# A linear-attention and two-MLP kernel: weight units confined to chunks 2 to 4, casts pinned to later steps, first weights converted in two parts

## The chip, the core and the metric

The kernel runs on one core of a Trainium2 chip, as one program from inputs in memory to outputs in memory. The metric is the device time of that program in microseconds. Of the engines, TensorE (PE) multiplies matrices, VectorE (DVE) and ScalarE (ACT) do elementwise work, GpSimd (POOL) and SyncE (SP) mostly issue DMAs. Each engine works through its own list of instructions in order and waits on semaphores of the others.

## What is computed

Three layers, one after the other, on 4 x 576 = 2304 tokens of width 512. Q, K and V have 8 heads of 64; the weights of both MLPs come in 64-bit floats and are turned to 32 bits on the chip.

```python
def _attn_ref(q, k, v):                       # each head, each batch
    q_s = exp(q - max(q, -1)); q_s /= sum(q_s, -1) + 1e-09
    k_s = exp(k - max(k, 2));  k_s /= sum(k_s, 2) + 1e-09      # over the sequence
    kv = einsum('bhsd,bhse->bhde', k_s, v)
    return einsum('bhsd,bhde->bhse', q_s, kv)

def _moe_ref(x, w_in, w_out, s, b):           # first MLP, 512 -> 2048 -> 512
    r = maximum(x @ w_in, 0.0)
    return (s * (r * r) + b) @ w_out

def _moe2_ref(x, w_in, w_out):                # second MLP, 512 -> 2048 -> 512
    h = x @ w_in
    return (h * tanh(softplus(h))) @ w_out
```

## The kernel before

**Chunks and steps.** The tokens are cut into five chunks of 512, 256, 512, 512 and 512 (chunks 0 to 4). Per chunk the attention of four pairs of heads (hp 0 to 3) gives four x tiles, and the first MLP then runs in 16 steps of 128 of its 2048 inner columns: step n is one h (a matmul group over four x tiles, kk 0 to 3), a relu and a square on ScalarE, and one y group into four accumulators. So there are 80 steps, 16 to a chunk. The attention of the next chunk is spread over the steps of this one. After the last chunk the second MLP runs on pairs of chunks, with products P1 to P7 of half blocks (seven multiplications of blocks in place of eight), and a rest.

**Halves.** A 32-bit matmul is done in three passes: each operand is split into a rounded high part and the remainder, by a cast on ScalarE and a subtraction on VectorE (`split`, L170 and L167). Names show it: xh and xl, gh and gl, kvh and kvl. Only the first steps of chunk 0 multiply whole operands (t, x), because their weights have not been split yet: h up to step 8, y up to step 6.

**Weights of the first MLP.** A pair of 128 x 512 blocks j is loaded by SP (`load_w`, tiles raw), its 64-bit words are turned to 32 bits by `bits` (L129 on ScalarE, then L130, L133, L137 and L141 on VectorE, in place in tile t), and later split into w. Tile t of j lies where the raw words of j - 1 were.

**Units.** The weights of the second MLP are cut into 32 units. A unit is one load of 512 KB (`unit_load`, tile ur, L302), the same five `bits` steps on a 512-wide tile u, four sums of blocks (L313), two casts and two subtractions into one tile umem, and two stores by GpSimd (L326, to wdi or wdo). `STARTS` holds the half step at which each unit begins: three from step 23 on, in chunk 1, and 29 over steps 32 to 78. The later ring of weight tiles (rw, `ring_load` on GpSimd's queue) reads back what the units stored.

**Second MLP's x.** In the last chunk `b_next` is called seven times for each of two k halves (tiles b_0 and b_1), from step L0 + 1 and from L0 + 7; L0 is the first step of the last chunk. Each call combines y blocks and splits one operand into xoP.

**What sets the order.** The program hands its instructions to a scheduler that orders each engine's list by a modelled time. `pin` and `keep_in_program_order` keep an instruction at its place in the program on its engine; unit casts, unit bits and the relus from step 23 (`U1`) on are pinned, x casts, kv casts and xoP casts are not. `at(step, kind, fn)` puts work into steps; within a step `run` names the kinds in order.

## Time and profile before

| | us |
|---|---|
| median of 3 runs | 865.53 (864.23 to 865.64) |
| the profiled execution | 868.49, its span 866.7 |
| TensorE busy | 828.4 (96%) |
| VectorE busy | 616.9 (71%) |
| ScalarE busy | 440.8 (51%) |
| GpSimd busy | 109.3 (13%) |
| mean granted TensorE clock | 0.988 of full |

The busy times are sums over the span, and the engines work beside each other. The granted clock is what the chip gave TensorE: 1.00 is 2.4 GHz and 0.50 is 1.2 GHz. A timeline row's bracket tells how long its engine had been idle before it and whose work ended that. The chunks follow each other in the span: chunk 0 until about 147 us, chunk 1 until about 213, chunks 2 to 4 until about 495, then the second MLP.

### The profile page before, as it was taken

The numbers are of one execution on the slowest core, as the hardware profiler recorded it, in microseconds if no ns is written. First come the engines' busy times: TensorE is split into PE (matmuls) and PEld (weight loads), VectorE is DVE, ScalarE is ACT, GpSimd is POOL, SyncE is SP. The second block draws the span as 40 slices with busy tenths as digits, with TensorE's granted clock in tenths as the row PEclk, the third lists the DMA queues.
The fourth block names the chain that finished last, engine by engine and source line by source line (L and its number), as shares of the span: only waits on it lengthen the run. The fifth ranks groups of instructions, "written<-read, shape, count | busy, mean of one in ns | idle before, by whom it ended". The sixth has DMA issues, their size and how long they took to land.

```text
span 866.7 us, 11570 instructions
## 1 busy us (share of the span) xinstructions
PE 828.4 (96%) x4084; PEld 666.0 (77%) x4084; DVE 616.9 (71%) x1153; ACT 440.8 (51%) x786; POOL 109.3 (13%) x196
## 2 busy tenths in 40 slices
PE   3799999998999999999989999989999999999998
PEld 2344787987888888888868878868788888878897
DVE  6989997568888887766887448687864655786511
ACT  3645777547666666555765435255442333544322
POOL 4000000000011001120212211101111111112110
PEclk9899999998999999999999999999999999999999
DMA  6994123144666556456656889657678866687891
GB/s 170 311 376 143 27 66 112 54 103 149 207 199 205 191 196 220 165 182 216 217 186 202 272 244 374 201 189 242 220 233 281 250 177 223 217 280 262 255 375 68
DMA packets 90474, 179.02 MB, mean 207 GB/s; under 512 B 26928, under 2 KB 45104, under 8 KB 86832
## 3 DMA queue, kind: packets, MB, share of 16 engines
q0 software_dynamic: 30256, 112.73, 40.0%
q1 hardware_dynamic: 59072, 64.50, 24.2%
q10 hardware_dynamic: 1088, 1.05, 0.4%
q8 instruction: 32, 0.52, 0.3%
q14 instruction: 26, 0.21, 0.1%
HBM read 131.60 MB, written 46.66 MB: 206 GB/s over the span
## 4 chain that ended last, share of the span: by engine, by line
PE 69%; DVE 13%; DMA 11%; SPq 2%; issue 2%; ACT 2%; POOL 0%; DVEq 0%; ACTq 0%; POOLq 0%
PE P L177 22%; PE h L177 16%; PE y L177 16%; PE rh L177 3%; PE ry L177 3%; DMA q<-in_q_dram 2%; DMA raw<-in_moe_w_out_dram 2%; DVE g L348 2%; DMA kb<-in_k_dram 2%; DVE w L167 1%; DVE gly_P L167 1%; PE P3y L177 1%; PE P5y L177 1%; PE P7y L177 1%; PE P4y L177 1%
## 5 line engine op out<-in xcount | busy, mean ns | idle before, releaser
L177 PE MATMUL h<-xh,w 128*128 128x512 f32 (+1 forms) x568 | 177.6, 378 | 7.8 <-ACT r L240 4.2
L177 PE MATMUL y<-gh,w 128*128 128x512 f32 (+1 forms) x584 | 176.6, 369 | 0.0
L177 PE MATMUL P<-xoP,rw 128*128 128x512 f32 x672 | 155.2, 390 | 1.0 <-DMA rw<-wdi 1.0
L177 PEld LDWEIGHTS P<-xoP,rw 128*128 128x128 f32 x672 | 125.8, 188 | 27.3 <-issue 1.4
L177 PEld LDWEIGHTS h<-xh,w 128*128 128x128 f32 x568 | 106.2, 194 | 26.6 <-ACT r L240 4.9
L177 PEld LDWEIGHTS y<-gh,w 128*128 128x128 f32 x584 | 106.5, 188 | 17.8
L170 ACT CAST ghy_P<-g 128x512 fp32r<-128x512 f32 x112 | 69.7, 623 | 82.4 <-DVE gly_P L167 34.7
L455 DVE TENSOR_TENSOR s<-s,P 128x512 f32<-128x512 f32 x112 | 75.2, 684 | 47.7 <-PE P L177 38.3
L177 PE MATMUL h<-xl,w 128*128 128x512 f32 (+1 forms) x284 | 106.7, 376 | 0.4 <-DVE xl L167 0.4
L177 PE MATMUL y<-gl,w 128*128 128x512 f32 (+1 forms) x292 | 106.8, 369 | 0.0
L167 DVE TENSOR_TENSOR gly_P<-g,ghy_P 128x512 fp32r<-128x512 f32 x112 | 75.8, 688 | 40.1 <-ACT ghy_P L170 39.2
L177 PE MATMUL P<-ghy_P,rw 128*128 128x512 f32 x224 | 87.2, 391 | 0.0
L458 ACT ACTIVATE g<-s 128x512 f32<-128x512 f32 x64 | 39.9, 631 | 81.7 <-DVE s L455 81.4
L170 ACT CAST umem<-u 128x512 fp32r<-128x512 f32 x64 | 37.4, 619 | 51.4 <-DVE u L313 45.5
L177 PEld LDWEIGHTS h<-xl,w 128*128 128x128 f32 x284 | 55.1, 194 | 9.7 <-DVE xl L167 0.6
L177 PEld LDWEIGHTS y<-gl,w 128*128 128x128 f32 x292 | 55.0, 188 | 9.0 <-DVE gl L167 0.2
L240 ACT ACTIVATE r<-h 128x512 f32<-128x512 f32 (+1 forms) x80 | 44.0, 550 | 31.0 <-PE h L177 26.4
L167 DVE TENSOR_TENSOR gl<-r,gh 128x512 fp32r<-128x512 f32 (+1 forms) x73 | 45.7, 628 | 14.3 <-ACT gh L170 14.2
L167 DVE TENSOR_TENSOR umem<-u,umem 128x512 fp32r<-128x512 f32 x64 | 42.1, 685 | 9.9 <-ACT umem L170 9.6
L177 PEld LDWEIGHTS P<-ghy_P,rw 128*128 128x128 f32 x224 | 42.1, 188 | 8.2
L243 ACT ACTIVATE r<-r 128x512 f32<-128x512 f32 (+1 forms) x80 | 47.0, 588 | 1.9
L177 PE MATMUL P<-gly_P,rw 128*128 128x512 f32 x112 | 45.2, 404 | 2.1 <-DVE gly_P L167 1.7
(181 smaller groups left out, 1299.1 us busy)
## 6 DMA issues: line engine op xcount, KB each, us to landing
rw<-wdo POOLq DMA_DIRECT2D x28, 1024.0 KB, 5.1
wdi<-umem POOLq DMA_DIRECT2D x32, 512.0 KB, 3.6
wdo<-umem POOLq DMA_DIRECT2D x32, 512.0 KB, 4.3
rw<-wdi POOLq DMA_DIRECT2D x16, 1024.0 KB, 6.6
rw<-wdi POOLq DMA_DIRECT2D x16, 768.0 KB, 6.0
raw<-in_moe_w_in_dram SPq DMA_DIRECT2D x16, 512.0 KB, 10.0
raw<-in_moe_w_out_dram SPq DMA_DIRECT2D x16, 512.0 KB, 10.8
ur<-in_moe_w_in_dram SPq DMA_DIRECT2D x16, 512.0 KB, 4.1
```

The lines of the kernel that those rows point to most:

```text
L167: eng.tensor_tensor(out=lo, in0=src, in1=hi.bitcast(F32), op=ALU.subtract)
L170: pin(nc.scalar.copy(out=hi, in_=src))
L177: mm = nc.tensor.matmul(out=ps, lhsT=x, rhs=y, start=start, stop=stop)
L240: op = nc.scalar.activation(out=r, in_=h_ps.pop(m), func=AF.Relu)
L243: nc.scalar.activation(out=r, in_=r, func=AF.Square)
L348: nc.vector.tensor_tensor(out=t.rearrange("p (a b) n -> p b a n", b=2)[:, 1], in0=t[:, 1:3], in1=t[:, 0:1].to_broadcast([P, 2, CM]), op=AL ...
L455: nc.vector.tensor_tensor(out=out, in0=a, in1=b, op=ALU.add)
L458: nc.scalar.activation(out=g[:, spot], in_=src, func=AF.Mish)
```

## The change

It has five parts. All 32 units start in steps 32 to 77, evenly, 1.44 steps apart where it was 1.59, so that none but the loads and sums of the first lie in chunk 1; relus are pinned from step 32 on. The first four x casts and kv casts, with their subtractions, are pinned: one x pair at each of h steps 5 to 8 (it was all four at step 8, free to move), and one kv pair at each of steps 3 to 6 (it was 0 to 3, free). The first weights are turned by two calls of `bits`, each on one of the two blocks. The casts of the second MLP's x are pinned and begin at L0 + 2 and L0 + 7. The ring's first tiles are taken in another order and loaded at L0 + 6, 10 and 14.

```diff
-        bits(t, w_raw.pop(j))
+        raw = w_raw.pop(j)
+        if j:
+            bits(t, raw)
+        else:
+            for i in range(2):
+                bits(t[:, i], raw[:, i])
...
-    def minus(eng, lo, src, hi):
-        eng.tensor_tensor(out=lo, in0=src, in1=hi.bitcast(F32), op=ALU.subtract)
-
-    def split(hi, lo, src, eng=None, pin=lambda ins: None):
+    def minus(eng, lo, src, hi, pin=lambda ins: None):
+        pin(eng.tensor_tensor(out=lo, in0=src, in1=hi.bitcast(F32), op=ALU.subtract))
+
+    def split(hi, lo, src, pin=lambda ins: None, pin_lo=lambda ins: None):
         pin(nc.scalar.copy(out=hi, in_=src))
-        minus(eng or nc.vector, lo, src, hi)
+        minus(nc.vector, lo, src, hi, pin_lo)
...
     U0 = 2 * NF
-    U1 = U0 - 9
-    STARTS = [2 * U1, 2 * U1 + 6, 2 * U1 + 12] + [2 * U0 + 2 * (NS - 2 - U0) * e // 29 for e in range(29)]
+    STARTS = [2 * U0 + 2 * (NS - 2 - U0) * e // 32 for e in range(32)]
...
-        if m >= U1:
+        if m >= U0:
             tc.keep_in_program_order(op)
...
-        split(x_op[r][:, 0, kb], x_op[r][:, 1, kb], src)
+        split(x_op[r][:, 0, kb], x_op[r][:, 1, kb], src, pin=pin)
...
-    RING = ("ws0", "last", "ws1")
+    RING = ("last", "ws0", "ws1")
...
             if c == 1:
-                at(hp, "att1", kv_hi, 0, hp)
-                at(hp, "att1", kv_lo, 0, hp)
+                at(hp + 3, "att1", kv_hi, 0, hp, pin)
+                at(hp + 3, "att1", kv_lo, 0, hp, pin)
...
-    at(U1 - 3, "load", unit_load, 0)
+    at(U0 - 4, "load", unit_load, 0)
...
-            at(L0 + 1 + 6 * kb + i, "unit", b_next, kb)
-    for s in (9, 11, 13):
+            at(L0 + 2 + 5 * kb + i, "unit", b_next, kb)
+    for s in (6, 10, 14):
         at(L0 + s, "load", ring_load)
...
-            if m == H_WHOLE - 1:
-                for kk in range(NK):
-                    x_t[0, kk] = tuple(t[:, 0:CHUNKS[0]] for t in x_tiles(kk, f"0_{kk}"))
-                    split(*x_t[0, kk], x_whole[kk])
+            if H_WHOLE - 1 - NK < m < H_WHOLE:
+                kk = m - H_WHOLE + NK
+                x_t[0, kk] = tuple(t[:, 0:CHUNKS[0]] for t in x_tiles(kk, f"0_{kk}"))
+                split(*x_t[0, kk], x_whole[kk], pin, pin)
```

`kv_hi` and `kv_lo` pass their new argument on to the cast and to the subtraction. Lines behind L170 stand four or five lines further down in the changed kernel (L240 is L244).

Three places show what the scheduler makes of it. On ScalarE at the start, before the first weights (t_295, from raw_172), the list before was this; xh, kvh are casts of x and kv halves, q_2 an exponential.

```order
L170 CAST xh_0_642<-x_247 128x512
L795 CAST kvh_1_464<-kvb_129 128x128
L745 ACTIVATE q_2_146<-q_2_146 128x640
L838 COPY x_293<-x_1_291 128x512
L816 COPY qt_341<-qt_2_331 128x512
L170 CAST xh_1_646<-x_293 128x512
L129 ACTIVATE t_295<-raw_172 128x1024
L810 ACTIVATE kvb_141<-kv_2_320,rs_2_336 64x64 x2
L795 CAST kvh_2_489<-kvb_141 128x128
```

And now:

```order
L842 COPY x_247<-x_0_245 128x512
L814 ACTIVATE kvb_129<-kv_1_268,rs_1_284 64x64 x2
L820 COPY qt_289<-qt_1_279 128x512
L749 ACTIVATE q_2_146<-q_2_146 128x640
L129 ACTIVATE t_295<-raw_172 128x512
L842 COPY x_293<-x_1_291 128x512
L820 COPY qt_346<-qt_2_336 128x512
L129 ACTIVATE t_295<-raw_172 128x512
L814 ACTIVATE kvb_141<-kv_2_325,rs_2_341 64x64 x2
```

The x and kv casts are gone from between, and the weights are cast in two pieces of 512 with other work between them.

The second place is the end of chunk 1. On SP, the loads around q of the first pair of heads of chunk 2 (q_0) before:

```order
L673 DMA vb<-in_v_dram 128x4x64 x2
L677 DMA vb<-in_v_dram 64x2x64
L653 DMA kb<-in_k_dram 128x2x256
L657 DMA kb<-in_k_dram 64x2x64
L302 DMA ur_1683<-in_moe_w_in_dram 128x2x512
L691 DMA q_0_1962<-in_q_dram 112x2x256
L691 DMA q_0_1962<-in_q_dram 16x2x256
```

And now:

```order
L677 DMA vb<-in_v_dram 128x4x64 x2
L681 DMA vb<-in_v_dram 64x2x64
L657 DMA kb<-in_k_dram 128x2x256
L661 DMA kb<-in_k_dram 64x2x64
L695 DMA q_0_1928<-in_q_dram 112x2x256
L695 DMA q_0_1928<-in_q_dram 16x2x256
L677 DMA vb<-in_v_dram 128x4x64 x2
L681 DMA vb<-in_v_dram 64x2x64
L657 DMA kb<-in_k_dram 128x2x256
L661 DMA kb<-in_k_dram 64x2x64
L306 DMA ur_2157<-in_moe_w_in_dram 128x2x512
```

The unit's load (ur) stood ahead of q_0 and now follows the next k.

There also, on ScalarE, from the q exponential on to the first relu behind the boundary; xn_3 and xh_3 are the last x tile of chunk 2 and its cast. Before:

```order
L821 CAST qth_3_2010<-qt_3_1976 128x512
L740 ACTIVATE q_1_2257<-q_1_2257 128x512
L170 CAST umem<-u_1859 128x4x128 x2
L850 COPY xn_3_2067<-x_3_2060 128x512
L170 CAST xh_3_2099<-xn_3_2067 128x512
L129 ACTIVATE u_2027<-ur_1865 128x512
L240 ACTIVATE r_2052<-h_2039 128x256
```

And now:

```order
L825 CAST qth_3_1976<-qt_3_1942 128x512
L744 ACTIVATE q_1_2208<-q_1_2208 128x512
L283 ACTIVATE ys_1_2128<-y_16_1317,bsum,sb_s 128x256
L854 COPY xn_3_2023<-x_3_2016 128x512
L175 CAST xh_3_2049<-xn_3_2023 128x512
L283 ACTIVATE ys_1_2136<-y_16_1319,bsum,sb_s 128x256
L244 ACTIVATE r_2078<-h_2065 128x512
```

The two unit casts (umem) ahead of xn_3 are gone; a y column (ys_1) stands there.

The third place is the last chunk, on ScalarE, between two relus. Before:

```order
L243 ACTIVATE r_4145<-r_4145 128x512
L170 CAST gh_4146<-r_4145 128x512
L170 CAST umem<-u_4077 128x4x128 x2
L170 CAST xoP_4223<-b_0_4072 128x512
L170 CAST xoP_4223<-b_1_4180 128x512
L129 ACTIVATE u_4164<-ur_4083 128x512
L170 CAST xoP_4277<-b_0_4072 128x512
L170 CAST xoP_4277<-b_1_4180 128x512
L170 CAST xoP_4313<-b_0_4072 128x512
L170 CAST xoP_4313<-b_1_4180 128x512
L170 CAST umem<-u_4164 128x4x128 x2
L240 ACTIVATE r_4204<-h_4191 128x512
```

And now:

```order
L244 ACTIVATE r_4127<-h_4114 128x512
L247 ACTIVATE r_4127<-r_4127 128x512
L175 CAST gh_4128<-r_4127 128x512
L129 ACTIVATE u_4146<-ur_4070 128x512
L175 CAST xoP_4160<-b_0_4059 128x512
L175 CAST umem<-u_4146 128x4x128 x2
L244 ACTIVATE r_4187<-h_4174 128x512
L247 ACTIVATE r_4187<-r_4187 128x512
L175 CAST gh_4188<-r_4187 128x512
L129 ACTIVATE u_4206<-ur_4152 128x512
L175 CAST xoP_4219<-b_0_4059 128x512
L175 CAST umem<-u_4206 128x4x128 x2
```

Where six xoP casts and four unit casts stood between one relu group and the next, one xoP cast and two unit casts do.

## Rows read from the trace of the kernel before

**Rows 1.** Windows view: each engine's busy time (x instructions), PEclk, DMA share, GB/s.

```profile
40.00:140.00 100.00, 99.92 (x405) 63.19 (x405) 91.03 (x136) 62.50 (x95) 0.21 (x2) 1.00 0.45 151
147.41:150.83 3.42, 3.05 (x14) 3.05 (x15) 2.03 (x6) 2.38 (x6) 0.00 (x0) 0.50 0.70 222
212.27:219.09 6.82, 6.26 (x15) 4.83 (x16) 6.20 (x15) 5.17 (x10) 1.04 (x2) 0.50 0.68 237
220.00:436.00 216.00, 216.00 (x1046) 178.13 (x1045) 169.68 (x377) 132.29 (x235) 28.41 (x46) 1.00 0.62 203
440.96:444.37 3.41, 3.04 (x7) 2.46 (x8) 2.01 (x5) 2.70 (x6) 1.50 (x2) 0.50 0.67 235
```

**Rows 2.** Timeline at the start: start, length, instruction xcount [idle before, releaser].

```profile
17.89 1.53 SPq L117 DMA_DIRECT2D raw<-in_moe_w_in_dram  x3
DMA to landing us min/median/max: 5.8/8.1/10.0
25.25 1.15 ACT L129 ACTIVATE t<-raw 128x1024 f32<-128x1024 f32 x1 [0.92 <-DMA raw<-in_moe_w_in_dram]
30.27 1.22 DVE L141 SCALAR_TENSOR_TENSOR t<-raw,t 128x1024 int32<-128x1024 int32 x1
31.54 7.00 PE L215 MATMUL h<-x,t 128*128 128x512 f32 x12 [2.16 <-DVE t L141]
```

**Rows 3.** Timeline of VectorE and TensorE, chunk 0, h steps 6 and 7.

```profile
65.28 2.35 DVE L141 SCALAR_TENSOR_TENSOR t<-raw,t 128x1024 int32<-128x1024 int32 x2
73.13 1.22 DVE L141 SCALAR_TENSOR_TENSOR t<-raw,t 128x1024 int32<-128x1024 int32 x1
76.46 3.60 PE L215 MATMUL h<-x,t 128*128 128x512 f32 x8
```

**Rows 4.** Timeline of TensorE, chunk 0 to 1: first, last of four gaps.

```profile
144.11 0.38 PE L177 MATMUL h<-xl,w 128*128 128x256 f32 x1 [0.36 <-DVE xl L167]
...
147.78 0.80 PE L177 MATMUL h<-xh,w 128*128 128x256 f32 x2 [0.79 <-ACT xh L170]
```

**Rows 5.** Timeline of VectorE and TensorE in chunk 1, columns as in rows 2.

```profile
192.28 0.69 DVE L724 TENSOR_REDUCE qm<-q 128x8 f32<-128x512 f32 x1 [3.23 <-DMA q<-in_q_dram]
...
194.50 0.63 PE L788 MATMUL qt<-ident,qn 128*128 128x128 f32 x4 [1.56 <-DVE rs L807]
197.01 0.39 PE L177 MATMUL h<-xh,w 128*128 128x256 f32 x1 [1.40 <-ACT r L240]
```

**Rows 6.** Timeline of ScalarE and TensorE at chunk 1 to 2.

```profile
210.52 1.12 ACT L170 CAST umem<-u 128x512 fp32r<-128x512 f32 x2
211.55 0.58 ACT L850 COPY xn<-x 128x512 f32<-128x512 f32 x1
212.16 0.62 ACT L170 CAST xh<-xn 128x512 fp32r<-128x512 f32 x1
...
212.83 0.79 PE L177 MATMUL h<-xh,w 128*128 128x512 f32 x1 [2.82 <-ACT xh L170]
```

**Rows 7.** Timeline of ScalarE and TensorE in the last chunk.

```profile
438.53 1.14 ACT L170 CAST xoP<-b 128x512 fp32r<-128x512 f32 x2 [3.62 <-PE y L177]
440.69 0.59 ACT L240 ACTIVATE r<-h 128x512 f32<-128x512 f32 x1
...
427.91 0.39 PE L177 MATMUL h<-xl,w 128*128 128x512 f32 x1
428.13 0.39 PE L177 MATMUL h<-xh,w 128*128 128x512 f32 x1
...
441.33 0.79 PE L177 MATMUL h<-xh,w 128*128 128x512 f32 x1 [2.84 <-ACT r L240]
```

**Rows 8.** Tile u: DVE, ACT busy in a window; step ns (min/median/max).

```profile
220.00:436.00 216.00, 103.59 (x229) 41.98 (x69) 1.00 0.62 203
L130 DVE TENSOR_SCALAR u<-u x32: 411/426/631, 182.4 to 483.7; 128x512 f32<-128x512 f32 x32
L137 DVE SCALAR_TENSOR_TENSOR u<-ur,u x32: 679/692/696, 183.4 to 485.1; 128x512 int32<-128x512 int32 x32
```

More of the change, by code (lines that the diff above doesn't have):

```diff
@@ L789, in att4_mm, with kv_hi @@
         qT_ps[c, hp] = ps[:, 0:n]
[L791 removed]
+    def kv_hi(b, hp, pin=lambda ins: None):
         hi = ap.tile([P, P], F32R, tag="kvh", bufs=NP + 1, name=f"kvh{b}_{hp}")
```

7 lines of the change are left out of this document (3 added, 4 removed).

## Prediction

> **What bounds the kernel now.** I read the stretches first (busy time of each engine, granted clock), then TensorE's own timeline for the places where it stood still, and behind each gap the timeline of the engine that it waited for. From 220 to 436 us TensorE is busy for all of 216.00 us at a granted clock of 1.00, while VectorE has 169.68 us of work there and ScalarE 132.29 [rows 1]. So the middle of the kernel is bound by matmuls, and a change to casts and loads can win only where TensorE stands still or runs at the lower of its two clock levels (1.2 in place of 2.4 GHz, granted 0.50). Up to 495 us those places are few: the start, before the first h at 31.54 [rows 2]; the change from chunk 0 to 1 [rows 4]; two stalls in chunk 1 [rows 5]; the change from chunk 1 to 2 [rows 6]; and one stall in the last chunk [rows 7]. At three of them the clock then falls to 0.50 for 3.42, 6.82 and 3.41 us [rows 1]; of the busy 3.05, 6.26 and 3.04 us there about half, 1.5, 3.1 and 1.5 us, is what the lower level costs. After 495 us the order hardly differs between the two kernels; I take nothing there, plus or minus 1.
>
> The sum is made against the profiled execution, 868.49 us, which is 2.96 above the median of 865.53; the forecast subtracts the same 2.96.
>
> **First weights in two parts, x and kv halves later: 1.0 us.** The first half lands 5.8 us after its issue at 17.89, so at 23.7; the cast that needs both halves starts only at 25.25, and the last bit step starts at 30.27 [rows 2]. Now the first half is cast alone: ScalarE about 0.7, more than half of the whole cast's 1.15 [rows 2], and VectorE 0.43 + 0.43 + 0.69 + 0.69 = 2.24 by the unit's 512-wide steps, two forms of which stand in [rows 8]. From about 24.0 that gives 26.9, and with some 1.5 of other short steps between them (an estimate) 28.4, or 3.1 before 31.54. The bounds are 26.9 and 31.5. The four x casts and kv casts that stood in this queue are gone from it, so the steps between are short.
>
> Most of that is given back. The casts come to about 61 to 86 us, where VectorE turns bits into weights one after the other, and q and k of the second batch land earlier, so that their steps are moved ahead too. The weights for h step 6 were done at 65.28 + 2.35 = 67.63 and those for step 7 at 73.13 + 1.22 = 74.35, 6.7 us later [rows 3]. Now the list between them holds more: a k maximum, an x and a kv half, two q steps and both long steps of another weight (2.35, [rows 3]). By the durations of the same forms that is 10.1 us, an estimate. With step 6's weights at 64.9 that makes 75.0 for step 7, which TensorE, 3.1 us early, would want at 76.46 - 3.1 = 73.4. It waits 1.6, and at step 8 I estimate 0.4 to 0.5 more. Net 1.0; bounds 3.1 and, if the list runs later still, -1.
>
> A rule speaks against the two parts. Each 512-wide long step takes 0.69 where the 1024-wide takes 1.22 [rows 2, 8], so four pairs cost about 4 x 0.16 = 0.6 us more, which is inside the 28.4. The Trainium skill, page Perfetto Trace Analysis, section Optimizing Scalar/DVE Operations, says that each operation pays a fixed access overhead of about 60 ns on VectorE and that larger operations help a saturated engine; by it four more instructions would be 0.24 us (an estimate). The rows show the larger price, and neither decides the sum.
>
> **Chunk 0 to 1: 2.5 us.** TensorE stands still four times between 144 and 148 us, 0.36 at the first and 0.79 at the last, 2.08 us together, waiting for x halves and q halves of the new chunk, and then loses 1.5 to the clock [rows 1, 4]: 3.6 in all. These come from VectorE's and ScalarE's lists, whose attention steps now begin some 10 us earlier, since q and k of head 2 and 3 no longer queue behind eight weight loads on SP. I take 2.5; bounds 0 and 3.6.
>
> **Chunk 1: 3.0 us.** At 192.28 VectorE has waited 3.23 us for q of chunk 2; a reciprocal queued behind it releases TensorE 1.56 us late at 194.50, and ScalarE's relu, late by the same wait, costs 1.40 at 197.01 [rows 5]. SP had issued a unit's 512 KB load just ahead of that q. Now the q load stands behind k and v alone, the unit's load three groups later, and no unit is converted in chunk 1 but the sums of the first. I take all 2.96; bounds 1.4 and 3.0.
>
> **Chunk 1 to 2: 5.0 us.** ScalarE casts two unit halves (1.12) and only then x of head 3 (0.58 and 0.62); TensorE waits 2.82 and then works 6.82 us at 0.50 [rows 1, 6]. The unit casts now stand three relu groups later. What stays ahead of x is a q exponential and a y column, some 0.9 us of lateness that I take as the new stall (bounds 0.3 and 2.8), because six y matmuls and two thirds of the second h are put in as cover. Gain 1.9, and 3.1 if the clock does not fall. I take it that it stays up, since the gaps of 1.56 and 1.40 in chunk 1, two in 4 us, left it at 1.00. By the Trainium skill, page TensorE: Matmul & The Clock Gate, section Part 1: The HAM clock gate, only the two levels exist, so this part is had whole or not at all; the trace agrees with its 0.50 and 1.00.
>
> **Last chunk: 4.3 us.** ScalarE starts two second-MLP casts at 438.53 after an idle 3.62, then two unit casts, and only then the relu for which TensorE has waited 2.84 at 441.33 [rows 7]; 1.5 of clock follows. The casts were free to drift together, two k halves at a time. Now they are pinned, one in most steps, each behind the step's relu. Bounds 0 and 4.3.
>
> **Three more units in chunks 2 to 4: -2.0 us.** A unit is 103.59 / 23 = 4.5 us of VectorE and 41.98 / 23 = 1.8 us of ScalarE [rows 8]. Three of them are 13.5 and 5.5 us over some 280 us, which raises VectorE from 79% to about 83% there. TensorE is saturated, and casts have slack: the relu that began at 440.69 was ready when its h ended, at 428.13 + 0.39 = 428.5, and would have been in time some 2.8 before, so over 9 us were free [rows 7]. But both lists are in order and now more of them is pinned; I set one stall of about 2 us, bounds 0 and 4.3 (one like [rows 7] with its clock). Their loads join SP's queue and their stores POOL's, ahead of nothing that is late there now. Of the three ring loads on POOL two come earlier and one a step later; that one stands behind one or two more unit stores, and what it brings is used only after 495 us, so I cost it at nothing; if it came late, it would be within the plus or minus 1 above.
>
> The sum: 1.0 + 2.5 + 3.0 + 5.0 + 4.3 - 2.0 = 13.8. 868.49 - 13.8 = 854.7 in a profiled run, 851.7 as a median; I say 852.
>
> **Rivals.**
> A, one stall moves: the clock still falls at the change to chunk 2 (3.1) and one full stall with its clock comes in chunks 2 to 4 (4.3 in place of 2.0, with another 2 elsewhere). For it: pinned casts cannot step aside. Against: 216 us without a gap while 23 units ran. It gives 852 + 3.1 + 4.3 = 859.
>
> B, little arrives before chunk 2: the start is given back entirely (1.0), the lists are as late at chunk 1 as before (2.5), and chunk 2 begins with the old stall (5.0). For it: VectorE is busy for 91.03 of the 100 us from 40 on [rows 1], and work was moved into that stretch. Against: the two unit loads and casts named in [rows 5, 6] are simply not there any more. It gives 852 + 8.5 = 860.5, up to 863.
>
> C, slower: ScalarE becomes the bound in chunks 2 to 4. A unit whose bit cast and two unit casts follow each other without a relu between holds ScalarE for its 0.7, VectorE's 2.24 and four short sums, and the two casts' 1.1, together 5 to 6 us, about a step of 24 matmuls 0.22 apart (427.91 to 428.13, [rows 7]), 5.4; every second unit is of that kind, in both kernels. Relus wait behind it. Two units now come in 2.9 steps instead of 3.2. If such a pair needs over 0.9 us more than its 2.9 steps, the 9 us of slack are gone after some ten of the sixteen pairs, and all later ones go onto TensorE: at 1.9 us over per pair, 30 - 9 = 21 us are lost. Then 852 + 21 = 873; it turns slower from some 15 us lost. Against: 132.29 of 216 us is far from full [rows 1]; for: the old stall at 441 is this mechanism, with casts added.
>
> **How the numbers follow.** A run of this kernel can tell about 0.2%, 1.7 us, from no change. Forecast 0.60, A 0.17, B 0.12, C 0.11. Faster by over 0.2%: all of the first three but a little, 0.86; within 0.2%, between B and C, 0.04; slower 0.10. The range: at the low end the start keeps its 3.1 (2.1 more), chunk 1 begins clean (1.1) and the units cost nothing (2.0), 846.5; at the high end A and most of B, 861.
>
> **What would show it.** First h at about 28.4, not 31.5; a wait of 1 to 2 us before h step 7; the VectorE wait for q near 190 gone with both gaps; the gap before the last quarter of chunk 2's first h under 1 us and a granted clock of 1.00 after it; no gap by a relu between 430 and 450. Wrong, if a relu holds TensorE for over 2 us anywhere between 220 and 490, if the granted clock falls there, or if chunk 1 ends with a gap as before.

## The result and the profile after

The changed kernel takes 876.49 us (median of 4 runs, 874.9 to 879.41), the kernel before 865.13 in the same session (864.23 to 865.64): a ratio of 1.0136, 95% interval 1.0108 to 1.0165. It is slower by 11.4 us, where 13.8 fewer were forecast. The profiled executions (879.41 and 868.49) lie 10.9 apart, so the two traces hold the difference and can be compared place by place.

| | before | after |
|---|---|---|
| TensorE busy, us | 828.4 | 832.9 |
| VectorE busy, us | 616.9 | 620.8 |
| ScalarE busy, us | 440.8 | 437.9 |
| mean granted clock | 0.988 | 0.986 |

No engine has become the bound. The time went into single stalls. The table gives where TensorE stood in the program, by the start of an h step: after minus before, in us of the profiled executions (positive is later).

| up to | h step | after minus before | gained in the stage | forecast |
|---|---|---|---|---|
| start | 10 | +0.15 | -0.15 | +1.0 |
| change to chunk 1 | 22 | +4.25 | -4.1 | +2.5 |
| chunk 1 and change to chunk 2 | 42 | -3.75 | +8.0 | +8.0 |
| chunk 2 and change to chunk 3 | 64 | +6.67 | -10.4 | a share of -2.0 |
| last chunk, start of the second MLP | second pair of chunks | +11.0 | -4.3 | +4.3, and 0 after 495 |

Each stage is read from one execution of each kernel, and executions differ. Two of the runs below, a_ring and a_xop, have the changed kernel's instructions in the same order on every engine until 463 and 425 us. At h step 64 they are 1.16 and 2.46 behind, not 6.67, and from step 42 on they lose 7.0 and 7.7, not 10.4. All three have the same gap of 2.54 us at the change to chunk 3. Behind it the granted clock was 0.50 for 6.8 us in the changed kernel (317.2 to 324.0) and for 3.4 in a_ring (314.4 to 317.8), and it stayed at 1.00 in a_xop (310 to 330). The kernel before took 860.58 to 869.72 in its 103 runs beside the experiments, with a median of 861.96 in the 16 runs whose mean granted clock was 0.995 or more and of 866.64 in the 14 with 0.988 or less; its profiled execution, 868.49 at 0.988, is among the slowest.

The stretches of the changed kernel (columns as in [rows 1]: length, busy time of TensorE, of its weight load, of VectorE, ScalarE and GpSimd, granted clock, DMA share, GB/s):

```profile
143.00:158.00 15.00, 10.15 (x52) 9.21 (x51) 9.30 (x20) 9.45 (x21) 0.20 (x2) 0.66 0.38 125
166.00:214.00 48.00, 47.56 (x406) 45.47 (x404) 29.84 (x75) 27.11 (x65) 0.89 (x9) 1.00 0.27 71
220.00:436.00 216.00, 209.97 (x992) 170.69 (x991) 162.45 (x360) 122.60 (x223) 27.76 (x46) 0.98 0.59 198
312.00:326.00 14.00, 11.24 (x38) 8.53 (x37) 11.12 (x24) 7.79 (x14) 1.16 (x3) 0.76 0.43 145
```

Chunk 1 is clean, as forecast: 47.56 of 48 us at a clock of 1.00. But the stretch from 220 to 436, which was full before [rows 1], now lacks 6.0 us, and VectorE and ScalarE did less work in it than before, since fewer steps fall into it (992 matmuls for 1046); 2.8 of the 6.0 and a low clock lie around the change to chunk 3, and the change to chunk 1 is worse than before.

**The start.** TensorE, the first h and the wait before h step 7:

```profile
27.38 1.99 PE L219 MATMUL h<-x,t 128*128 128x512 f32 x4
74.92 5.33 PE L219 MATMUL h<-x,t 128*128 128x512 f32 x8 [2.43 <-DVE t L141]
```

The first h comes 4.2 before that of [rows 2]. TensorE then waits 2.43 for weights 7, and its eight matmuls take 5.33 where those of [rows 3] took 3.60; the mean granted clock was 0.55 from 75.3 to 78.6.

**The change to chunk 1.** VectorE, then TensorE:

```profile
145.94 0.69 DVE L728 TENSOR_REDUCE qm<-q 128x8 f32<-128x512 f32 x1 [2.48 <-DMA q<-in_q_dram]
146.54 1.22 DVE L172 TENSOR_TENSOR w<-t,w 128x1024 fp32r<-128x1024 f32 x1
147.68 0.42 DVE L172 TENSOR_TENSOR qtl<-qt,qth 128x256 fp32r<-128x256 f32 x1
...
144.99 0.30 PE L182 MATMUL x<-qth,kvh 128*128 128x64 f32 x1 [1.17 <-ACT qth L825]
148.15 0.42 PE L182 MATMUL x<-qtl,kvh 128*128 128x64 f32 x1 [2.86 <-DVE qtl L172]
150.43 0.80 PE L182 MATMUL h<-xh,w 128*128 128x256 f32 x2 [0.68 <-ACT xh L175]
```

VectorE waits 2.48 for a q of chunk 2, whose attention is not due before chunk 1. The subtraction qtl, for which TensorE waits 2.86, is ready and stands behind it.

**The change to chunk 3.** SyncE's queue, VectorE, ScalarE and TensorE:

```profile
303.86 0.37 SPq L306 DMA_DIRECT2D ur<-in_moe_w_in_dram  x1
307.20 0.37 SPq L695 DMA_DIRECT2D q<-in_q_dram  x1
...
306.42 0.76 DVE L763 TENSOR_TENSOR qn<-q,qs 128x256 f32<-128x256 f32 x2
312.40 0.69 DVE L728 TENSOR_REDUCE qm<-q 128x8 f32<-128x512 f32 x1 [0.99 <-DMA q<-in_q_dram]
314.80 0.69 DVE L729 TENSOR_TENSOR q<-q,qm 128x512 f32<-128x512 f32 x1
...
315.52 0.63 ACT L744 ACTIVATE q<-q 128x512 f32<-128x512 f32 x1 [4.76 <-DVE q L729]
316.13 1.14 ACT L175 CAST umem<-u 128x512 fp32r<-128x512 f32 x2
317.17 0.59 ACT L244 ACTIVATE r<-h 128x512 f32<-128x512 f32 x1
...
317.81 0.80 PE L182 MATMUL h<-xh,w 128*128 128x512 f32 x1 [2.54 <-ACT r L244]
```

One chain runs through all four. The q tiles have two buffers, and this is chunk 4's attention, due in chunk 3. The products qn at 306.42 free one, and only then can SyncE issue the load of the next q, 5.17 us long, beside a unit's load and two of its stores. VectorE, ScalarE (idle 4.76), two unit casts and a relu follow. Of the 4.76 only 0.99 is VectorE's wait for the transfer; for the rest VectorE works through two x halves and a unit's bit step that stand between its two q steps. (The relu is that of step 47, whose last matmul ended at 306.16; it frees the accumulator for which TensorE waits at 317.81.) The kernel before has the same order on ScalarE there, the q exponential and two unit casts ahead of the relu, but no unit ahead of those products on VectorE:

```profile
300.95 0.37 SPq L691 DMA_DIRECT2D q<-in_q_dram  x1
304.81 0.37 SPq L302 DMA_DIRECT2D ur<-in_moe_w_in_dram  x1
```

Its q landed at 304.54, and nothing waited.

The relu is not the whole of the stage. Of the 10.4 us lost between h steps 42 and 64 some 4 are lost by step 48, ahead of it. There ScalarE, then TensorE:

```profile
279.40 0.66 ACT L129 ACTIVATE u<-ur 128x512 f32<-128x512 f32 x1 [1.34 <-DMA ur<-in_moe_w_in_dram]
279.96 0.28 ACT L799 CAST kvh<-bd 128x128 fp32r<-128x128 f32 x1
...
280.29 0.30 PE L182 MATMUL x<-qth,kvh 128*128 128x64 f32 x1 [1.54 <-ACT kvh L799]
```

A unit's bit cast waits 1.34 for its load, and a kv cast that TensorE needs stands behind it.

**The end.** Two gaps of TensorE, and GpSimd's queue:

```profile
472.13 1.62 PE L182 MATMUL P<-xoP,rw 128*128 128x512 f32 x6 [2.48 <-DMA rw<-wdi]
518.01 4.34 PE L182 MATMUL P<-xoP,rw 128*128 128x512 f32 x11 [3.43 <-DMA rw<-wdi]
...
506.88 1.50 POOL L330 DMA_DIRECT2D wdo<-umem  x2 [8.24 <-DVE umem L172]
510.72 1.42 POOL L417 DMA_DIRECT2D rw<-wdi  x2 [2.35 <-DVE xoP L172]
```

Both gaps wait for ring loads. The old gap of [rows 7] is gone, but relus behind unit casts cost 0.56 at 413 and 1.61 at 453.

### The profile page after: what moved, and what is told of

It is laid out like the page before. It is cut to its first block, busy times and chain, and to the rows that moved or that the text cites. A ratio compares the mean times of both kernels' runs of the same rounds, so it can differ in the third digit from the quotient of the medians.

```text
span 877.6 us, 11572 instructions
## 1 busy us (share of the span) xinstructions
PE 832.9 (95%) x4084; PEld 667.5 (76%) x4084; DVE 620.8 (71%) x1157; ACT 437.9 (50%) x787; POOL 109.1 (12%) x196
## 4 chain that ended last, share of the span: by engine, by line
PE 57%; DVE 16%; DMA 14%; issue 5%; ACT 4%; SPq 2%; POOL 1%; DVEq 0%; POOLq 0%; ACTq 0%
PE P L182 22%; PE h L182 10%; PE y L182 8%; DMA q<-in_q_dram 3%; PE rh L182 3%; PE ry L182 3%; DMA kb<-in_k_dram 2%; DMA ur<-in_moe_w_out_dram 2%; DMA raw<-in_moe_w_out_dram 2%; DVE g L352 2%; DMA b<-yd 1%; DVE gly_P L172 1%; PE P3y L182 1%; PE P5y L182 1%; PE P7y L182 1%
## 5 line engine op out<-in xcount | busy, mean ns | idle before, releaser
L182 PE MATMUL P<-xoP,rw 128*128 128x512 f32 x672 | 157.4, 393 | 5.9 <-DMA rw<-wdi 5.9
L459 DVE TENSOR_TENSOR s<-s,P 128x512 f32<-128x512 f32 x112 | 75.3, 686 | 43.7 <-PE P L182 34.1
L244 ACT ACTIVATE r<-h 128x512 f32<-128x512 f32 (+1 forms) x80 | 43.9, 549 | 24.5 <-PE h L182 13.4
L172 DVE TENSOR_TENSOR gl<-r,gh 128x512 fp32r<-128x512 f32 (+1 forms) x73 | 45.7, 629 | 14.1 <-ACT gh L175 13.8
```

The source lines that it names most:

```text
L172: pin(eng.tensor_tensor(out=lo, in0=src, in1=hi.bitcast(F32), op=ALU.subtract))
L182: mm = nc.tensor.matmul(out=ps, lhsT=x, rhs=y, start=start, stop=stop)
L244: op = nc.scalar.activation(out=r, in_=h_ps.pop(m), func=AF.Relu)
L459: nc.vector.tensor_tensor(out=out, in0=a, in1=b, op=ALU.add)
```

## The experiments

All ratios are to the kernel before, which was run beside each. Labels with a_ start from the changed kernel, with b_ and c1 from the kernel before. "Behind" and "ahead" are positions against the profiled execution of the kernel before, which is 3.4 to 5.2 above its medians beside the runs; so only changes of position along a run are read, and those to some 2 or 3 us.

| run | ratio | 95% interval |
|---|---|---|
| the changed kernel | 1.0136 | 1.0108 to 1.0165 |
| a_pinq | 1.0035 | 1.0010 to 1.0059 |
| a_starts | 1.0087 | 1.0056 to 1.0119 |
| a_even | 1.0050 | 1.0027 to 1.0072 |
| a_odd | 1.0267 | 1.0232 to 1.0303 |
| a_xkv | 1.0078 | 1.0051 to 1.0106 |
| a_whole | 1.0098 | 1.0073 to 1.0122 |
| a_ring | 1.0089 | 1.0059 to 1.0118 |
| a_xop | 1.0172 | 1.0142 to 1.0202 |
| a_even_ring | 1.0021 | 1.0002 to 1.0041 |
| b_starts | 1.0034 | 1.0015 to 1.0052 |
| b_even | 0.9978 | 0.9957 to 0.9999 |
| b_even_xop | 0.9995 | 0.9977 to 1.0013 |
| b_even_xop3 | 0.9987 | 0.9968 to 1.0006 |
| b_pinq | 0.9986 | 0.9963 to 1.0008 |
| c1 | 1.0044 | 1.0026 to 1.0062 |
| c1_early | 1.0123 | 1.0103 to 1.0142 |
| c1_pinq | 0.9945 | 0.9925 to 0.9964 |
| c1_pinq_xop | 0.9962 | 0.9941 to 0.9984 |

### q steps held back

**a_pinq**

```diff
-        nc.vector.tensor_reduce(out=mx, in_=t, axis=AX.X, op=ALU.max)
+        op = nc.vector.tensor_reduce(out=mx, in_=t, axis=AX.X, op=ALU.max)
+        if c > 1:
+            pin(op)
...
-        nc.scalar.activation(out=q_in[c, hp], in_=q_in[c, hp], func=AF.Exp)
+        op = nc.scalar.activation(out=q_in[c, hp], in_=q_in[c, hp], func=AF.Exp)
+        if c > 1:
+            pin(op)
```

> The changed kernel with one thing more: from chunk 2 on, the q maximum on VectorE and the q exponential on ScalarE are held behind the instruction that the program has before them on their engine, so that they cannot be moved ahead of a chunk's end. Theory Q (a q step that waits for its transfer stands ahead of urgent casts and relus at two chunk changes): the gaps of 2.86 at 148.15 and of 2.54 at 317.81 go, with the half clock behind each (about 1.5 to 2 us); of the 4.2 lost by the change to chunk 1 some 3, of the 10.4 lost by the change to chunk 3 some 6 come back: 876.5 - 9 = 867 to 868. Theory U (32 units are simply too much for VectorE and ScalarE in chunks 2 to 4): the relu stays late by the unit's casts that stand ahead of it, and the time stays at 874 to 877.

867.88 us: 8.7 come back without a unit being moved. From h step 10 to 22 it falls behind by 0.6 (4.1 in the changed kernel), and from step 42 to 62 it loses nothing (7.0 to 10.4 in three executions of the changed order). ScalarE at the change to chunk 3 now goes from the x casts to the unit casts to the relu, with no q between, and TensorE has no gap over 0.4 there:

```profile
298.68 2.18 ACT L175 CAST xh<-xn 128x512 fp32r<-128x512 f32 x4
304.04 1.14 ACT L175 CAST umem<-u 128x512 fp32r<-128x512 f32 x2 [3.18 <-DVE u L317]
305.09 0.59 ACT L244 ACTIVATE r<-h 128x512 f32<-128x512 f32 x1
```

A new gap of 3.12 stands at 403.5: VectorE waits 1.95 there for a block of the second MLP's x, and a unit's casts and a relu follow late. Theory Q holds; U, that 32 units are too many, falls. The edit also moves other instructions on all of TensorE's, VectorE's and ScalarE's lists from about 125 us on, so the 8.7 are those of the whole new order.

**b_pinq** is the same edit in the kernel before.

> The kernel before with only the q maximum and q exponential held back from chunk 2 on; units, first weights, x, kv and the ring as before. The prediction put the stalls of 1.56 and 1.40 in chunk 1 and of 2.82 with its half clock at the change to chunk 2 down to unit loads and casts, which the change moves away. If it is the q steps that wait for their transfer there, as in the changed kernel at the two other chunk changes: these stalls go with the units left in place, 865 - 6 = 857 to 860. If the units are what delays them: 864 to 866.

862.46 us, a ratio that can't be told from 1. But the profile answers the question: from h step 22 to 44 it moves from 1.7 to 11.5 ahead, 9.8 gained, with the three units still in chunk 1. The old stalls of [rows 5, 6] need both, a unit and a q step that was moved ahead; either can be taken away. The expected time was missed, since part of the 9.8 belongs to the profiled execution of the kernel before (868.49, where the median beside this run was 863.26), and since 4.6 is lost again around 389.75:

```profile
388.28 0.49 DVE L359 TENSOR_SCALAR b<-b,bsum 128x512 f32<-128x512 f32 x1 [4.11 <-DMA b<-yd]
...
389.75 0.50 PE L177 MATMUL y<-gl,w 128*128 128x512 f32 x1 [2.45 <-DVE gl L167]
```

It is the same mechanism with another transfer: a first step on b waits 4.11 for its load, one of eight in flight, with gl behind it.

### The units' places

**a_starts** and **b_starts** exchange the starting steps (and the relus' first pinned step and the first unit load, which go with them) between the two kernels.

```diff
+    U1 = U0 - 9
-    STARTS = [2 * U0 + 2 * (NS - 2 - U0) * e // 32 for e in range(32)]
+    STARTS = [2 * U1, 2 * U1 + 6, 2 * U1 + 12] + [2 * U0 + 2 * (NS - 2 - U0) * e // 29 for e in range(29)]
```

> The changed kernel with the units' starting steps of the kernel before (three in chunk 1, 29 in chunks 2 to 4, relus pinned from step 23); all other parts as changed. If the moved units cause the loss of 10.4 at the end of chunk 2 and the stalls at 453, 472 and 518 (3.0, with 2.5 at 518), these go and the old stalls of chunk 1 come back (some 8): the change to chunk 1 stays 4.2 late, the last chunk keeps its gain of 4.3, so 865 to 867. If the other parts cause the loss (pins on x, kv and the second MLP's x), it stays at 874 or above.

870.84: between the two cases. Half of the loss came with the starts, and half stays without them: the change to chunk 1 costs 4.2 here too (1.7 ahead at step 10, 2.5 behind at 22), where no unit has begun. The end comes out otherwise: from h step 64 to the second pair of chunks a_starts gains 3.7, where the changed kernel loses 4.3. With the old starts TensorE is full in the last chunk, in spite of the pinned casts; from 436 to 490 first the changed kernel, then a_starts:

```profile
436.00:490.00 54.00, 49.91 (x220) 40.70 (x219) 42.55 (x85) 31.95 (x57) 10.56 (x15) 1.00 0.64 204
436.00:490.00 54.00, 54.00 (x240) 44.75 (x239) 45.63 (x93) 34.32 (x61) 10.45 (x14) 1.00 0.66 218
```

The last unit's stores are issued at 490.98 and the third ring load at 494.44, in the changed kernel at 506.88 and 510.72.

> The kernel before with the new starting steps of the units alone (32 over chunks 2 to 4, relus pinned from step 32). If the units cause what came after chunk 1: chunk 0 ends as before, chunk 1 gains some 8, the end of chunk 2 loses some 10, the last chunk keeps its old stall of about 4 and perhaps gains or loses one more: 866 to 870. If the units are harmless and the pinned casts do the harm: about 865.1 - 8 = 857.

867.43, as expected. Chunk 1 gains 8.0 (1.5 ahead at step 22, 9.5 at 42), and the change to chunk 3 takes 6.9 back (2.6 ahead at step 64) with the same gap of 2.54 by a relu. The new starts alone do both. At the end b_starts, with the free casts, loses only 0.9 from step 64 on.

**a_even** and **a_odd** put every unit on the first or the later half of a step.

```diff
-    STARTS = [2 * U0 + 2 * (NS - 2 - U0) * e // 32 for e in range(32)]
+    STARTS = [2 * (U0 + (NS - 2 - U0) * e // 32) for e in range(32)]
...
+    STARTS = [2 * (U0 + (NS - 2 - U0) * e // 32) + 1 for e in range(32)]
```

> The changed kernel with each unit's start rounded down to a whole step, so that a relu stands between its bit cast and its two casts in every one of the 32 units (16 of 32 stand without a relu between in the changed kernel). Theory C of the prediction (units without a relu between hold ScalarE too long): the stalls at 413, 453 and 317 go with their clock, 0.56 + 1.61 + 2.54 + 3.5, and the time is 867 to 869. Theory Q (q's transfer ends late): the load order on SyncE around the change to chunk 3 is the same, so that 6.0 stays, and only some 2 us of chunk 4 go: 873 to 875.

> The changed kernel with each unit's start moved to the later half of its step, so that in 31 of 32 units no relu stands between the bit cast and the two casts (16 in the changed kernel, 0 with whole steps, which gave 867.4). Theory C (such units hold ScalarE and make the relu late): about as much slower than the changed kernel as whole steps were faster, 883 to 890, with relus behind casts of u as the most frequent reason of TensorE's gaps in chunks 2 to 4. If only the places at the chunk changes matter (q's transfer, which other work meets there), the time is within 4 of 876.5, up or down.

867.41 and 887.72: with the same 32 units in the same chunks, half a step decides over 20 us. The stretch 220 to 436 of a_even:

```profile
220.00:436.00 216.00, 215.73 (x1025) 177.66 (x1025) 171.95 (x383) 128.76 (x231) 30.75 (x50) 1.00 0.63 212
```

and of a_odd:

```profile
220.00:436.00 216.00, 204.28 (x960) 165.64 (x960) 162.38 (x358) 118.10 (x217) 26.56 (x44) 0.98 0.58 195
```

On whole steps TensorE is as full as in [rows 1], with more work on VectorE; on half steps it lacks 11.7 us. So the rival's mechanism, a unit without a relu between, is real, but it does not act as a load that adds up: nearly all of the loss lies in few places (7.2 from h step 40 to 42, 13.8 from 46 to 52). On whole steps the stall at the change to chunk 3 is gone, although SyncE's and ScalarE's order there is the same: the unit ahead of the products stands half a step earlier, the q load is issued at 296.72 (and takes 4.94, hardly less than the 5.17), and the relu runs from 306.75 to 307.34, just in time for the h that begins at 307.39. There the two theories act on one place and a_even alone can't tell them apart; a_pinq does. The two edits were not tried together on the changed kernel; c1_pinq_xop comes nearest to that.

### The start

**a_xkv** takes the first x and kv halves back (free to move, x at h step 8, kv at steps 0 to 3); **a_whole** takes back the two parts.

```diff
-                at(hp + 3, "att1", kv_hi, 0, hp, pin)
-                at(hp + 3, "att1", kv_lo, 0, hp, pin)
+                at(hp, "att1", kv_hi, 0, hp)
+                at(hp, "att1", kv_lo, 0, hp)
...
-            if H_WHOLE - 1 - NK < m < H_WHOLE:
+            if m == H_WHOLE - 1:
```

> The changed kernel with the first x and kv halves as in the kernel before (not pinned, x at h step 8, kv at steps 0 to 3); the first weights still in two parts. If the pinned x and kv halves are what gave the early start back (the gap of 2.43 before h step 7 with the clock at 0.50 behind it) and what left VectorE behind at the change to chunk 1: the gap near 75 falls below 1, the position at h step 10 is 2 to 3 ahead of the kernel before and not 0.1 behind, and of the 4.2 lost by the change to chunk 1 some 2 to 3 come back: 871 to 873. If weights 7 come as late without them (VectorE works off one list either way), it stays at 875 to 877.

```diff
-        if j:
-            bits(t, raw)
-        else:
-            for i in range(2):
-                bits(t[:, i], raw[:, i])
+        bits(t, raw)
```

> The changed kernel with the first weights turned as one, as in the kernel before; x and kv halves still pinned later. If the two parts give the 3 to 4 us of earlier start and the pins of x and kv lose them again before h step 7, the start is now as late as before (first h at 31 to 32) and the gap before step 7 stays: position at h step 10 some 2 to 4 behind the kernel before, and 878 to 880. If the early start itself makes the gap (VectorE has the same list to work off, so TensorE waits for weights 7 at the same moment either way), the gap near 75 is gone and the time is 875 to 877.

871.49 and 873.46: each edit taken away makes the kernel faster, though a_whole's interval overlaps the changed kernel's. At h step 10 the changed kernel is 0.15 behind, a_xkv 3.7 ahead, a_whole 2.1 ahead, and neither has a gap near 75. Each of the two parts brings TensorE forward by itself; together VectorE cannot follow, and TensorE waits 2.2 to 4.0 before h step 7 in the eight runs that have both. In three of them (a_starts, a_even, a_even_ring) the clock stays up behind that wait, and they are 1.7 to 2.2 ahead at step 10; in the other five it falls to 0.50 there, and they are between 0.1 ahead and 2.0 behind. The lists are the same in all eight up to there. (The five b_ runs, which have the kernel before's lists there, are 0.3 to 1.1 ahead of its profiled execution.) Neither run gets back what the change to chunk 1 takes: from step 10 to 22 a_xkv loses 4.5 and a_whole 6.1. So a_whole is only 0.3 better than the changed kernel at step 22, and its gain in time isn't shown to come from the start. My expectation for a_whole, a loss at the start, was wrong in both its cases; its time was met by neither.

### The second MLP's x and the ring

**a_ring** takes the ring back, **a_xop** the pinned casts.

```diff
-    RING = ("last", "ws0", "ws1")
+    RING = ("ws0", "last", "ws1")
...
-    for s in (6, 10, 14):
+    for s in (9, 11, 13):
```

> The changed kernel with the ring's first tiles and its three loading steps (9, 11, 13 of the last chunk) as in the kernel before; only GpSimd's list differs from the changed kernel. If the early first ring load slows the unit's load beside it (6.04 us from issue to landing, where 3.8 is usual) and so makes the relu of the gap of 2.48 at 473 late, that gap goes; if the last ring loads then also come before the second MLP wants them, the 3.43 at 518 falls to about 1: together 2.5 to 5 us, 871.5 to 874 against the 876.5 of the changed kernel. If the ring is harmless and the last units set both (their stores stand ahead of the third ring load either way), 875 to 877.

```diff
-        split(x_op[r][:, 0, kb], x_op[r][:, 1, kb], src, pin=pin)
+        split(x_op[r][:, 0, kb], x_op[r][:, 1, kb], src)
...
-            at(L0 + 2 + 5 * kb + i, "unit", b_next, kb)
+            at(L0 + 1 + 6 * kb + i, "unit", b_next, kb)
```

> The changed kernel with the casts of the second MLP's x as in the kernel before (free to move, from L0 + 1 and L0 + 7). The pinned casts removed the old gap of 2.84 and its half clock in the last chunk (4.3 by the prediction). If they are worth that, it comes back: 879 to 881. If the pin takes its own gain back, because the last pinned subtraction of b_1 frees the tile of the third ring load late (in the changed kernel that load is issued at 510.7, right behind it, and TensorE waits 3.43 for it at 518): the third load comes earlier, the gap at 518 falls to 1, and the two cancel: 874 to 877.

a_ring 873.11, some 3.3 faster, but its interval overlaps the changed kernel's, and the traces don't put the gain down to the ring: the lists are the same until 463 us, a_ring is 6.4 better than the changed kernel at h step 74, which begins about there, and 6.7 at the end. So 0.4 comes behind the edit, and no loss by the ring's new order is shown. The gap of 2.48 has another mechanism than I expected. The early first ring load let six P matmuls stand early in TensorE's list, and TensorE waits 2.48 for that load at 472.13; in a_ring the first of them has 0.88 before it, at 480.84. The gap at the second MLP's start stays, 3.57 at 510.5, there for VectorE, so the ring did not make that one. a_xop takes 878.02, and its interval overlaps the changed kernel's: the old gap is back (3.33 at 445.8, 2.24 at 456.4), and the one at 518 has become 1.89 at 529.9. Whatever the pinned casts give and take is too little to tell here.

**a_even_ring** has the edits of a_even and a_ring; **b_even** is b_starts on whole steps, the kernel before with 32 units over chunks 2 to 4 and nothing else.

```diff
-    STARTS = [2 * U0 + 2 * (NS - 2 - U0) * e // 32 for e in range(32)]
+    STARTS = [2 * (U0 + (NS - 2 - U0) * e // 32) for e in range(32)]
```

> The changed kernel with all units on whole steps and the ring as in the kernel before. With whole steps alone TensorE came to the second MLP 10 us ahead of the kernel before in the profiled executions, and lost 3.00 at 498.8 for a ring load and 2.98 at 514.5 for VectorE, which waited for data from memory. If the ring's order makes these two: 867.4 - 6 = 861 to 863. If the last unit's stores and the second half of the second MLP's x decide when the third ring load can be issued, then a faster chunk 4 only waits longer there: 866 to 868.

> The kernel before with 32 units over chunks 2 to 4, all on whole steps (a relu between the bit cast and the two casts of each); no other part of the change. The new starts alone gave 867.4, with gaps of 2.54 at 310 and 3.28 at 439. If units without a relu between make those gaps: both go with their clock, 867.4 - 8 = 859 to 861, and it beats the kernel before. If they come from transfers and casts that are merely near, one of the two stays: 863 to 866.

**b_even_xop** is b_even with the pinned casts, from L0 + 2 and L0 + 7; **b_even_xop3** has their second half from L0 + 5.

```diff
-        split(x_op[r][:, 0, kb], x_op[r][:, 1, kb], src)
+        split(x_op[r][:, 0, kb], x_op[r][:, 1, kb], src, pin=pin)
...
-            at(L0 + 1 + 6 * kb + i, "unit", b_next, kb)
+            at(L0 + 2 + 5 * kb + i, "unit", b_next, kb)
...
+            at(L0 + 2 + 3 * kb + i, "unit", b_next, kb)
```

> The kernel before with 32 units on whole steps in chunks 2 to 4 (862.7, with a gap of 4.26 at 434.5 by casts of the second MLP's x) and, in addition, these casts pinned as in the change. If the pin gives its gain: 862.7 - 5 = 857 to 859. If the third ring load waits for the last pinned subtraction of b_1 and TensorE for that load: the gap at 434 goes, and one of 2.5 to 4 comes at the second MLP's start: 861 to 863.

> The same with the second half of these casts from L0 + 5 in place of L0 + 7, so that the last pinned subtraction of b_1 stands two steps (some 11 us) earlier and the third ring load has only the last unit's stores ahead of it. If b_1's tile is what held that load: it is issued right behind the stores and the gap at the second MLP's start falls to 0 to 1: 2 to 3 us below the kernel with L0 + 7, 856 to 859. If the stores or the load itself hold it, the two are equal within 1 us. If two x casts and a unit in one step make a relu late, it is slower than the one with L0 + 7.

866.57, 862.70, 863.16 and 863.85. a_even_ring's interval overlaps a_even's, and from the first ring load on the two traces move apart by only some 0.2. b_even just beats the kernel before: no gap over 0.5 from 150 to 430, but one of 4.26 at 434.5 by the free casts, which I had thought would go. With the pin (b_even_xop) that gap is 0.47, TensorE is 13.1 ahead at step 74 (6.8 in b_even), and at the fourth group of products of the second MLP (P_0_3) 5.3 ahead (7.3): all given back, and more. In a_even_ring the third ring load waits for the last pinned step on b_1, whose tile it fills:

```profile
491.23 0.68 DVE L172 TENSOR_TENSOR xoP<-b,xoP 128x512 fp32r<-128x512 f32 x1
492.21 1.42 POOL L417 DMA_DIRECT2D rw<-wdi  x2 [2.26 <-DVE xoP L172]
```

In b_even_xop3 it does not wait (issued at 487.77, right behind the stores), and TensorE stands still all the same, 1.82 and 3.30 us:

```profile
496.85 12.78 PE L177 MATMUL P<-xoP,rw 128*128 128x512 f32 x48 [1.82 <-DMA rw<-wdi]
512.93 7.32 PE L177 MATMUL P<-xoP,rw 128*128 128x512 f32 x19 [3.30 <-DMA rw<-wdi]
```

So the tile is one holder, and by the trace the transfers are the next; no run has fewer of them.

### Both edits that help, together

**c1** is b_even with the first weights in two parts; **c1_early** spreads its units over 42 steps in place of 46; **c1_pinq** is c1 with the q steps held as in a_pinq; **c1_pinq_xop** adds the pinned casts, from L0 + 2 and L0 + 6.

```diff
-        bits(t, w_raw.pop(j))
+        raw = w_raw.pop(j)
+        if j:
+            bits(t, raw)
+        else:
+            for i in range(2):
+                bits(t[:, i], raw[:, i])
...
-    STARTS = [2 * (U0 + (NS - 2 - U0) * e // 32) for e in range(32)]
+    STARTS = [2 * (U0 + (NS - 6 - U0) * e // 32) for e in range(32)]
```

> The kernel before with 32 units on whole steps of chunks 2 to 4 and the first weights in two parts; x, kv, the second MLP's x and the ring as before. It joins the two parts of the change that the runs so far speak for. Whole steps alone gave a ratio of 0.9978; without the x and kv pins the changed kernel was 3.7 ahead of the kernel before at h step 10. If both gains keep and add, with some 1 given back at the change to chunk 1: 862.7 - 2.5 = 860, a ratio of 0.994 to 0.996. If the earlier start only makes VectorE later at the change to chunk 1 (there the two-part kernels were 0.35 to 0.8 behind the kernel before): no gain over 0.9978.

> The same with the 32 units ending four steps earlier (spread over 42 steps in place of 46). If the second MLP's start is held by the last units and the third ring load behind their stores, then TensorE's gaps between 490 and 520 are gone and 1 to 3 us come off: 857 to 859. If what holds it is the transfers themselves (y stores, second pair of x blocks and ring loads in flight together, 7 to 12 us each), ending earlier gives nothing there, and the denser units may cost a stall of 2 to 4 in chunks 2 to 4: 860 to 864.

> The first kernel of this group with the q maximum and the q exponential held behind the instruction that the program has before them, from chunk 2 on, as it was tried on the changed kernel (where 8.7 of 11.4 came back). If any q step still stands ahead of urgent work at a chunk change, 1 to 3 us come off: 857 to 859. If whole steps already leave no q step late there (TensorE had no gap over 0.5 between 212 and 430), it gives nothing, and pinned q steps wait behind relus: 860 to 863.

```diff
-            at(L0 + 1 + 6 * kb + i, "unit", b_next, kb)
+            at(L0 + 2 + 4 * kb + i, "unit", b_next, kb)
```

> The fastest kernel so far (units on whole steps, first weights in two parts, q steps held back: 859.8, with one gap over 1 us left in the chunks, 4.19 at 432 by the free casts of the second MLP's x) with these casts pinned, from L0 + 2 and L0 + 6. If the gap at 432 alone is to be had: 859.8 - 4 = 855 to 857. If TensorE, then some 13 us ahead of the kernel before, waits for the ring's and the second pair's transfers at the second MLP's start, as it did without the held q steps (1.8 and 3.3 there): no gain, 859 to 861.

c1, 867.87, is slower than b_even: two gains did not add. It is 3.8 ahead at step 10 and 0.2 behind at 22, since VectorE again waits for a q of chunk 2, 1.60 at 144.37, with urgent halves behind it. c1_early, 875.45, has seven gaps of 1.08 to 2.28 between 320 and 455: denser units cost more than c1 loses at the end. It has no gap from 490 to 520, but it comes there 6.7 behind, so it doesn't tell whether ending earlier would help. c1_pinq, 859.82, is the fastest, below both kernels (0.9945, 0.9925 to 0.9964): 4.2 ahead at step 10, 4.9 at 22, 11.6 at 42, 10.3 at 64. The stretch of the change to chunk 1 in c1:

```profile
143.00:158.00 15.00, 13.28 (x80) 12.51 (x80) 8.76 (x21) 8.33 (x22) 0.40 (x4) 0.69 0.26 81
```

and of c1_pinq, where the clock stays up:

```profile
143.00:158.00 15.00, 14.59 (x122) 13.56 (x123) 10.71 (x27) 9.26 (x23) 0.50 (x5) 1.00 0.30 89
```

One gap over 1 us is left in its chunks after the first, 4.19 at 432. c1_pinq_xop takes it away and is 14.4 ahead at the last h step, but 8.7 at P_0_3; 859.81 is no gain. From 490 to 520 it has 25.27 us of TensorE, against 29.59 in c1_pinq, and the DMA share is 0.97 and 1.00 there. First c1_pinq:

```profile
490.00:520.00 30.00, 29.59 (x131) 24.18 (x130) 18.61 (x29) 11.01 (x18) 4.94 (x7) 1.00 1.00 328
```

Then c1_pinq_xop:

```profile
490.00:520.00 30.00, 25.27 (x103) 19.84 (x102) 17.11 (x27) 12.29 (x20) 3.87 (x6) 0.94 0.97 331
```

Coming earlier, TensorE meets the same transfers and waits for them.

## Why the prediction was wrong, step by step

The time is 24.8 us above the forecast of 851.7. Three steps carry nearly all of that: the change to chunk 1 (6.6), the three more units (8.4), and the last chunk with what follows it (8.6). A smaller flaw is in the frame: the sum counts the low clock of the profiled execution as gain, and then subtracts the 2.96 by which that execution lies above the median; as far as those 2.96 are low clock, they are counted twice.

- **Chunk 1 and the change to chunk 2: right, 8.0 for 8.0**, and b_starts shows that the moved units gave it. The reason was half of it: b_pinq removes the same stalls without moving a unit. In [rows 5] VectorE waits for a q, and I asked what delayed the load (a unit's load ahead of it), not why a step that was not due stood ahead of urgent ones. The exact match is in part luck. I called the clock's share had whole or not at all, but it is had in parts: behind the same gap of 2.8 at the change to chunk 2 the kernel before has 6.8 us at 0.50, a_starts 3.4 (216.5 to 219.9), so up to 1.7 of the 8.0 belongs to one execution.
- **Chunk 0 to 1: the sign failed, 2.5 forecast, -4.1 measured.** I took q and k coming earlier as relief. Now a q step of chunk 2 stands a chunk too early ahead of urgent halves, and VectorE waits 2.48 there for a transfer. a_pinq against the changed kernel (0.6 lost for 4.1) and c1_pinq against c1 (0.7 gained for 4.0 lost) show it. The edits of the start bring it on, not the units: between h steps 10 and 22 the seven kernels with both edits and free q steps lose 2.9 to 4.2, the four with one of them 4.0 to 6.1, and the four with neither (b_starts and the b_even runs) gain 0.4 to 0.7. That the earlier q and k let the scheduler move the step is my reading. In a_whole no such wait of VectorE stands at the change, and what takes its 6.1 is open.
- **Start: 1.0 forecast, -0.15 measured, within its bounds; the wait was undersized and the clock left out.** First h at 27.38 (28.4 forecast), weights 7 at 74.78 (75.0), a wait of 2.43 (1.6). Behind it the clock fell, for which the sum has no term; where it stayed up, with the same lists, the two edits gain 1.7 to 2.2. Alone, the two parts gain 3.7 and the halves 2.1, so together they give less than the parts alone.
- **Three more units, -2.0 with bounds 0 and 4.3: mis-sized, -10.4 in the profiled execution and some 7 to 8 in two others.** I counted work (VectorE at 83%) and took slack from the best place, [rows 7]. What mattered was phase, and what stood beside the units at the change. a_even, with as many units, loses nothing between steps 42 and 64; a_odd loses 11.2; a_pinq, with the same starts, loses nothing either. A relu that holds TensorE for over 2 us was named as a sign of being wrong, and it came (2.54 at 317.81). Rival C, at 873, has the right sign and its unit without a relu between, but it priced a steady overload of ScalarE, which the runs do not show; that it lies near the measured time is in part chance.
- **Last chunk, 4.3: the gap of [rows 7] went, as forecast, and the time with it.** The step that failed is the one that costs the third ring load, behind one or two more unit stores, at nothing. In the changed kernel it is issued at 510.72, behind the last stores (506.88) and the last pinned step on b_1, whose tile it fills, and TensorE waits 3.43 for it. The pins alone do not do that: a_starts, with the pins and the old starts, gains 3.7 from step 64 to the second pair of chunks, near the 4.3 forecast, while every run with the new starts loses there, pinned or free (0.9 in b_starts to 11.0 in c1_early). With both, in b_even_xop, b_even_xop3 and c1_pinq_xop, 3 to 6 are gained from step 66 to the last h step and 6 to 9 lost from there to P_0_3. That the transfers at the start of the second MLP are what ends last there is read from the traces.

What stays open: how much of the end could be had with fewer bytes in flight there was not tried, and the gaps by steps on b (a_pinq at 403, b_pinq at 390) were read, not removed. A third q buffer, which would part the q load from the products, was not tried.

## What to carry to other kernels

Before a change to a list that a scheduler orders, look at each urgent place for steps that are not due, that wait for a transfer, and that stand ahead of the urgent ones; an edit that frees time can let more of them move ahead. Hold such steps back first, and then measure the rest: two parts that each gain can lose together, and one that gains nothing may do so only because what ends last is next door. Before a stage is read from two profiles, see how far two executions of the same lists lie apart in it (here up to 5.5 us by h step 64). With VectorE busy for some 80% of the time, as here, the phase of added work (half a step, 20 us) decided more than its amount (three units more).

## What the runs showed of the hardware

Of the 31 unit loads of 512 KB whose landing the changed kernel's trace shows, 25 landed 3.7 to 4.2 us after their issue, and one beside a ring load took 6.04; q's 256 KB took 3.59 us in the kernel before and 5.17 in the changed one, beside a unit load and two stores. The ring loads issued in the last chunk took 6.7 to 7.8 us in these two kernels; in c1_pinq those issued from 499 to 520 took 9.0 to 11.8, where the DMA share is 1.00 at 328 GB/s over 30 us (490 to 520).

Of TensorE's clock: gaps of 2.43, 2.86 and 2.54 us were each followed by a low stretch (means of 0.55 from 75.3 to 78.6, 0.51 from 147 to 157, 0.62 from 316 to 325), while after the 2.48 at 472 and the 1.61 at 453 it stayed at 1.00 (436 to 490). The length of a gap doesn't settle it: with the same lists, waits of 2.43, 2.77, 3.26, 3.52 and 3.99 before h step 7 were followed by a low stretch and waits of 2.23, 2.53 and 2.85 were not, and the same gap of 2.54 at the change to chunk 3 by 6.8, 3.4 and no us of it. A matmul group that took 3.60 at 1.00 took 5.33 behind the first of these.
